# 8 MB loads with 64 KB runs and a written order on VectorE and GpSimd, in a decode attention kernel

## The chip, the cores and the metric

The kernel runs on one core of one Trainium2 chip. The metric is the device time of the program in microseconds (us); lower is better. Executions of the kernel before agree within 0.04%.

TensorE is called PE below, and its weight loads PEld; VectorE is DVE, ScalarE is ACT, GpSimd is POOL, and SyncE is SP. SP issues the loads. The 16 DMA engines of the core move the bytes. A run is a stretch of bytes in a row for one partition; the trace records it as one packet. Each load ends with 4-byte packets, the semaphore writes that signal its landing. A drain is a time in which fewer than 16 engines have a packet to move.

## The reference

One decode step of attention over a large cache, mixed with a small gated MLP. Cut to what matters:

```
B, H, Sk, Dh, D, F = 4, 32, 8192, 128, 1024, 3584
q = x @ wq                                     # (4, 1, 4096)
scores = einsum("bhqd,bhkd->bhqk", q, k_cache) * Dh**-0.5
p = softmax(scores)
o = einsum("bhqk,bhkd->bhqd", p, v_cache)
a = o.reshape(4, 1, 4096) @ wo
b = x + r * ((silu(x @ w_gate) * (x @ w_up)) @ w_down)
out = g * a + (1 - g) * b
```

The K and V caches are 268.4 MB each. All that is read comes to 575.68 MB, and every byte is used once, so the time is set by how fast bytes come in.

## The kernel before

K and V come in tiles of 4 MB: two heads, 128 partitions, 32 KB in a row for each partition. Five such tiles are in flight or in use, in a ring of five buffers. For K, VectorE transposes each tile in four chunks and PE multiplies each chunk with weights `Z` made from the query, eight matmuls a chunk, into `S_ps`. After eight tiles (16 heads) a softmax follows on VectorE, GpSimd and ScalarE. Its weights go to `PB`, and eight tiles later PE sums V with them, 32 matmuls a tile.

```
ring = ctx.enter_context(tc.tile_pool(name="ring", bufs=5))
ctx.enter_context(tc.manual_schedule(engines={mybir.EngineType.PE}))   # the others: the scheduler's order
...
def k_piece(u):
    ...
    kn = slot()                                          # 4 MB, the next of five
    nc.sync.dma_start(out=kn[:], in_=kv_view(A_k_cache, u))
    for c in range(JR // CJ):                            # 4 chunks
        T = ttp.tile([P, CJ, 2, 32, 2], BF, name="T", tag="T")      # two buffers
        nc.vector.transpose(out=T..., in_=kn[:, c * CJ * Dh:(c + 1) * CJ * Dh]...)
        for he in range(4):
            for z in range(2):
                nc.tensor.matmul(sps[:, z, :], lhsT=Z[:, he, s:s + P], rhs=T[...], ...)
        if c == 0:
            flush()                                      # finish an earlier group of heads
    if t == GT - 1:
        softmax(g)
...
def v_piece(u):
    ...
    cut = 4 if u == NT - 1 else 1                        # the last tile in four parts of 1 MB
    ...                                                  # 32 matmuls into o_ps
    nc.scalar.activation(out=o_sb[:], in_=o_ps[:, 0, :], func=ACT.Copy, scale=mE[:, 0:1])
    nc.vector.scalar_tensor_tensor(out=o_sb[:], in0=o_ps[:, 1, :], scalar=mE[:, 1:2], in1=o_sb[:], ...)
...
order: k0 ... k7, then k8 v0 k9 v1 ..., at the end v alone; 2 MB of wo before the last V tile, 6 MB after it
```

## Time and profile before

| | before |
|---|---|
| device time, median | 1349.33 us |
| span in the profile | 1347.8 us |
| PE busy / VectorE busy | 79% / 47% |
| DMA engines busy | 99.5% |

From the page of the kernel before: the span; busy us of each engine with its share of the span; busy tenths and GB/s of the DMA in 40 equal slices; packets, MB and engine share of the load queue; the chain of waits by engine.

```profile
span 1347.8 us, 8253 instructions
...
PE 1059.3 (79%) x4600; PEld 233.2 (17%) x2412; DVE 631.4 (47%) x375; ACT 41.5 (3%) x46; POOL 47.9 (4%) x115
...
DMA  9999999999999999999999999999999999999997
GB/s 403 433 433 422 433 430 430 432 433 430 430 433 430 430 431 434 429 431 432 433 428 432 433 430 430 433 431 429 432 434 429 428 433 434 429 428 434 432 423 323
...
q1 hardware_dynamic: 22104, 575.68, 99.5%
...
DMA 50%; PE 30%; DVE 11%; issue 6%; ACT 1%; POOL 1%; SPq 0%; DVEq 0%; ACTq 0%
```

DMA stands at 9 tenths or more in every slice but the last. Nothing else does. The queue is the bound, and the idle time of the other engines costs nothing as long as the queue has work.

The DMA issues of the same page: destination and source, number, KB each, and the median time from issue to landing.

```profile
piece<-in_A_k_cache_dram SPq DMA_DIRECT2D x64, 4096.0 KB, 39.4
piece<-in_A_v_cache_dram SPq DMA_DIRECT2D x63, 4096.0 KB, 39.1
```

A 4 MB load takes 9.8 us at this rate (4.19 MB / 428 GB/s), but 39 us pass from its issue to its landing. Four loads stand in the queue at any time. That depth is the margin which this kernel has against delays in the compute.

The timeline of VectorE at the end of one softmax group (start, duration, instruction; in brackets how long the engine had idled and for what):

```profile
780.80 0.24 DVE L355 SCALAR_TENSOR_TENSOR mex<-mask,m,pen 128x16 f32<-128x16 f32 x1
787.26 0.75 DVE L412 SCALAR_TENSOR_TENSOR OS<-o_ps,mE,OS 128x512 f32<-128x512 f32 x1 [6.23 <-ACT OS L411]
788.03 0.17 DVE L360 TENSOR_TENSOR gmm<-gmx,nmask 128x16 f32<-128x16 f32 x1
```

Between `mex` and `gmm`, both softmax steps, the scheduler has put the correction `OS` of a V sum, which waits for PE and ScalarE.

And the last work of PE in its timeline:

```profile
1342.57 1.02 PE L188 MATMUL acc<-piece,LT 128*4 128x512 bf16 x4 [0.17 <-DMA piece<-in_A_wo_dram]
...
1343.81 1.02 PE L188 MATMUL acc<-piece,LT 128*4 128x512 bf16 x4 [0.22 <-DMA piece<-in_A_wo_dram]
```

The last wo matmuls wait for their data: the load queue holds the end. The last packet lands at 1343.34 us, and PE is done 1.5 us after.

### The profile page before, as it was taken

The page shows a single profiled execution, that of the slowest core. Times are in us where ns is not written, and L with a number is a line of the kernel's source. Part 1 is how long each engine was busy: PE and PEld are TensorE (multiplying, and loading weights), DVE is VectorE, ACT ScalarE, POOL GpSimd, SP SyncE. Part 2 cuts the span into 40 slices and gives each one's busy share as a digit, 9 for nine tenths or more (in the row PEclk, how much of TensorE's full clock was granted, in tenths as well). Part 3 has the DMA queues.
Part 4 walks back from the last instruction along what each step waited for, and adds up shares of the span by engine and source line. Part 5 has one row for each costly group of instructions (what it writes and reads, how often), then busy time and mean ns, then how long its engine had stood idle before and what let it go on. Part 6 is the DMA issues. An engine that isn't in the chain of part 4 may idle for free.

```text
span 1347.8 us, 8253 instructions
## 1 busy us (share of the span) xinstructions
PE 1059.3 (79%) x4600; PEld 233.2 (17%) x2412; DVE 631.4 (47%) x375; ACT 41.5 (3%) x46; POOL 47.9 (4%) x115
## 2 busy tenths in 40 slices
PE   2667779876978868876998769888788859797878
PEld 0111111211111111111212111211112112121111
DVE  3555755535544554454545454444544456346000
ACT  0000010001000010001000010000000010000000
POOL 2000000000000000000000000000000000000000
PEclk8878989898989989989898879899888979999899
DMA  9999999999999999999999999999999999999997
GB/s 403 433 433 422 433 430 430 432 433 430 430 433 430 430 431 434 429 431 432 433 428 432 433 430 430 433 431 429 432 434 429 428 433 434 429 428 434 432 423 323
DMA packets 22162, 576.22 MB, mean 428 GB/s; under 512 B 2399, under 2 KB 2407, under 8 KB 2925
## 3 DMA queue, kind: packets, MB, share of 16 engines
q1 hardware_dynamic: 22104, 575.68, 99.5%
q8 instruction: 27, 0.44, 0.1%
q14 instruction: 11, 0.08, 0.0%
q10 hardware_dynamic: 20, 0.02, 0.0%
HBM read 575.68 MB, written 0.01 MB: 427 GB/s over the span
## 4 chain that ended last, share of the span: by engine, by line
DMA 50%; PE 30%; DVE 11%; issue 6%; ACT 1%; POOL 1%; SPq 0%; DVEq 0%; ACTq 0%
DMA piece<-in_A_k_cache_dram 40%; PE o_ps L401 16%; PE S_ps L342 13%; DVE T L336 10%; DMA piece<-in_A_v_cache_dram 9%; PE small L419 1%; DMA piece<-in_A_wo_dram 1%; POOL PB L373 1%; DVE PT L367 1%; ACT PTs L365 1%; ACT OS L411 1%; DVE OS L412 1%; POOL tot L377 0%; PE acc L188 0%; PE o_ps L225 0%
## 5 line engine op out<-in xcount | busy, mean ns | idle before, releaser
L336 DVE STREAM_TRANSPOSE T<-piece 128x2048 uint32<-128x2048 uint32 x256 | 576.1, 2288 | 437.0 <-DMA piece<-in_A_k_cache_dram 321.1
L342 PE MATMUL S_ps<-T,Z 128*128 128x512 bf16 x2048 | 544.6, 416 | 246.6 <-DVE T L336 235.3
L401 PE MATMUL o_ps<-piece,PB 128*16 128x512 bf16 x2048 | 457.6, 382 | 14.8 <-DMA piece<-in_A_v_cache_dram 14.8
L342 PEld LDWEIGHTS <-Z 128*128 128x128 bf16 x1024 | 108.0, 105 | 667.2 <-issue 664.3
L401 PEld LDWEIGHTS <-PB 128*16 128x16 bf16 x1024 | 91.9, 90 | 373.1 <-issue 361.3
L412 DVE SCALAR_TENSOR_TENSOR OS<-o_ps,mE,OS 128x512 f32<-128x512 f32 x16 | 12.0, 751 | 174.6 <-ACT OS L411 174.6
L326 POOL TENSOR_TENSOR Z<-qa,mq 128x16 bf16<-128x16 bf16 x64 | 16.7, 262 | 1072.3 <-PE S_ps L342 1054.3
L411 ACT ACTIVATE OS<-o_ps,mE 128x512 f32<-128x512 f32 x16 | 11.0, 687 | 1040.5 <-PE o_ps L401 1040.5
L419 PEld LDWEIGHTS small<-selg,OS 128*128 128x128 f32 x128 | 24.9, 273 | 12.2 <-issue 11.1
L419 PE MATMUL small<-selg,OS 128*128 128x8 f32 x128 | 22.3, 302 | 0.0
L353 DVE TENSOR_REDUCE m<-S_ps 128x1 f32<-128x1024 f32 x8 | 9.8, 1225 | 15.9 <-PE S_ps L342 15.9
L188 PE MATMUL acc<-piece,LT 128*4 128x512 bf16 x64 | 14.9, 378 | 1.7 <-DMA piece<-in_A_wo_dram 1.6
L373 POOL COPY PB<-PT 64x1024 bf16<-64x1024 bf16 x8 | 15.1, 1884 | 29.1 <-DVE rex L375 29.1
L372 ACT COPY PB<-PT 64x1024 bf16<-64x1024 bf16 x8 | 15.3, 1908 | 10.6 <-DVE PT L367 10.6
L367 DVE STREAM_TRANSPOSE PT<-PTs 128x1024 bf16<-128x1024 bf16 x8 | 10.0, 1245 | 11.9 <-ACT PTs L365 11.9
L188 PE MATMUL acc<-piece,hT 128*4 128x512 bf16 x56 | 12.4, 379 | 0.0
L131 PE MATMUL small<-identb,x 6*128 6x6 bf16 x8 | 0.6, 194 | 14.2 <-DVE identb L128 14.2
L379 DVE RECIPROCAL rinv<-tot 128x16 f32<-128x16 f32 x8 | 2.0, 253 | 19.9 <-POOL tot L377 19.9
L365 ACT ACTIVATE PTs<-S_ps,negm 128x1024 bf16<-128x1024 f32 x8 | 8.9, 1113 | 70.0 <-DVE negm L362 70.0
L225 PE MATMUL S_ps<-piece,xw 128*4 128x512 bf16 x64 | 6.6, 591 | 3.0 <-DMA piece<-in_A_wq_dram 3.0
L422 DVE SCALAR_TENSOR_TENSOR OT<-small,sgb,rinv 128x8 bf16<-128x8 f32 x16 | 3.2, 202 | 11.7 <-PE small L419 11.7
L358 POOL PARTITION_ALL_REDUCE gmx<-mex x8 | 3.1, 390 | 81.9 <-issue 50.3
(72 smaller groups left out, 74.6 us busy)
## 6 DMA issues: line engine op xcount, KB each, us to landing
piece<-in_A_k_cache_dram SPq DMA_DIRECT2D x64, 4096.0 KB, 39.4
piece<-in_A_v_cache_dram SPq DMA_DIRECT2D x63, 4096.0 KB, 39.1
piece<-in_A_wq_dram SPq DMA_DIRECT2D x2, 4096.0 KB, 22.1
piece<-in_B_w_gate_dram SPq DMA_DIRECT2D x2, 3584.0 KB, 40.1
piece<-in_B_w_up_dram SPq DMA_DIRECT2D x2, 3584.0 KB, 34.6
piece<-in_A_wo_dram SPq DMA_DIRECT2D x6, 1024.0 KB
piece<-in_B_w_down_dram SPq DMA_DIRECT2D x1, 4096.0 KB, 35.6
piece<-in_A_v_cache_dram SPq DMA_DIRECT2D x4, 1024.0 KB, 32.6
```

What stands on the lines that cost most here:

```text
L188: nc.tensor.matmul(out_ap, lhsT=lhsT, rhs=rhs, start=start, stop=True, skip_group_check=True)
L326: nc.gpsimd.tensor_tensor(out=Z[:, :, 31:31 + P].rearrange("p e (s d c) -> p e s d c", s=HT, d=QH)[:, :, :, :, 0], in0=qa[:, :, h0:h0 + HT ...
L336: nc.vector.transpose(out=T[:].rearrange("p j h i e -> p (j h i e)").bitcast(U32), in_=kn[:, c * CJ * Dh:(c + 1) * CJ * Dh].bitcast(U32))
L342: nc.tensor.matmul(sps[:, z, :], lhsT=Z[:, he, s:s + P], rhs=T[:, 16 * z:16 * z + 16, half, :, e], start=(t == 0 and c == 0 and he == 0), ...
L365: nc.scalar.activation(out=PTs[:], in_=sps[:].rearrange("p z n -> p (z n)"), func=ACT.Exp, bias=negm[:, 0:1], scale=scale, accum_out=rs[:, ...
L367: nc.vector.transpose(out=PT[:].rearrange("p j i -> p (j i)"), in_=PTs[:])
L372: nc.scalar.copy(out=Bv[0:W, :, :, 0, :], in_=Pv[0:W])
L373: nc.gpsimd.tensor_copy(out=Bv[W:P, :, :, 1, :], in_=Pv[W:P])
L401: nc.tensor.matmul(o_ps[row:row + NM, e, :], lhsT=B_[:, JT * t + c, z, w].rearrange("p e s j -> p (e s j)"), rhs=vn[:, j0 * Dh:(j0 + 4) * ...
L411: nc.scalar.activation(out=o_sb[:], in_=o_ps[:, 0, :], func=ACT.Copy, scale=mE[:, 0:1])
L412: nc.vector.scalar_tensor_tensor(out=o_sb[:], in0=o_ps[:, 1, :], scalar=mE[:, 1:2], in1=o_sb[:], op0=ALU.mult, op1=ALU.add)
L419: nc.tensor.matmul(oT[:, :], lhsT=o_sb[:, q * Dh:(q + 1) * Dh], rhs=selg[:, q].rearrange("p t s -> p (t s)"), start=(q == 0), stop=(q == 3))
```

## The change

The intent is longer runs. Two tiles become a pair of 8 MB, four heads with 64 KB in a row for each partition, loaded by one transfer. The ring stays at five slots of 4 MB, so one pair in five wraps round the end and comes as two 4 MB transfers with 32 KB runs. VectorE and GpSimd keep the written order, in which the softmax steps come before the V sum. The last V pairs come in halves, and w_down is laid out in longer runs.

```diff
-    ring = ctx.enter_context(tc.tile_pool(name="ring", bufs=5))
-    ctx.enter_context(tc.manual_schedule(engines={mybir.EngineType.PE}))
+    ctx.enter_context(tc.manual_schedule(engines={mybir.EngineType.PE, mybir.EngineType.DVE, mybir.EngineType.Pool}))
+    ring = const.tile([P, NS, RING], BF, name="ring")          # NS = 5
+    def load_pair(src, n, apart=False):
+        a = slots(2)
+        if a + 1 < NS and not apart:
+            lo = a * RING
+            nc.sync.dma_start(out=flat[:, lo:lo + 2 * n], in_=src)
+            return [flat[:, lo:lo + n], flat[:, lo + n:lo + 2 * n]]
+        halves = [ring[:, a], ring[:, (a + 1) % NS]]
+        for i, half in enumerate(halves):
+            nc.sync.dma_start(out=half[:, 0:n], in_=src[:, i * n:(i + 1) * n])
+        return halves
...
-    return cache[b, h0:h0 + HT].rearrange("h (r j) d -> (h r) (j d)", j=JR)
+    return cache[b, h0:h0 + NQ].rearrange("h (r j) d -> (h r) (j d)", j=2 * JR)
...                                                       # k_pair: 8 chunks
+            if n == 0:
+                flush()          # PE: 8 products that finish a group of heads
+            if n == 2:
+                flush_late()     # VectorE: their scaling
...                                                       # v_pair: 64 matmuls
+        if d < ND - 1:
+            vs = load_pair(vv, RING, apart=d >= ND - 3)
+        else:                                             # first half whole, second in four parts
+            vs = [ring[:, slots(1)] for _ in range(2)]
+            nc.sync.dma_start(out=vs[0], in_=vv[:, 0:RING])
+            for c in range(4):
+                lo, hi = c * RING // 4, (c + 1) * RING // 4
+                nc.sync.dma_start(out=vs[1][:, lo:hi], in_=vv[:, RING + lo:RING + hi])
```

Heads are now finished in groups of 16 instead of 8, so at the end four wo blocks instead of two need the last V sum.

## The prediction

> **What bounds the kernel now.** The load queue. The span is 1347.8 us; the table of DMA queues gives queue 1 575.68 MB and 99.5% of the 16 engines' span, and the 40-slice table shows DMA at 9 tenths or more in every slice but the last, mostly 428 to 434 GB/s. In the packet records all 16 engines are active together for 1272 us, and packet time per engine sums to 1341.7 us: hardly any transfer time is idle. PE is busy 79%, VectorE 47%. Issue to landing of a 4 MB K load is 39.4 us, against some 9.8 us of transfer (4.19 MB at 428 GB/s): four loads are queued, so compute has about three loads of margin. The waits of VectorE (321 us for K loads) and PE (235 us for VectorE) are slack.
>
> **What the change gives.** Bytes stay. Median packet times in the trace: 4 KB 160 ns, 8 KB 312 ns, 28 KB 1062 ns, 32 KB 1215 ns. The line through first and last has a slope of 27.2 B/ns per engine (435 GB/s for 16) and 9 to 10 ns per packet. The slope is the fabric ceiling that the Trainium skill gives (DMA: Bandwidth & Descriptors, "Where 436 GB/s comes from"). Longer runs can only remove the per-packet part. By the code, 52 of 68 pairs go as one 8 (or 7) MB transfer with runs of 64 or 56 KB; one pair in five wraps round the five-slot ring and keeps 32 KB, as do the last V pairs; w_down goes from 8 to 28 KB runs. About 7,300 of 22,100 packets vanish: 7,300 x 9.5 ns / 16 = 4.3 us, plus about 0.6 us for some 1,000 semaphore writes of 9 ns. All of it is critical, because the queue is. Gain about 4.9 us, 0.4%.
>
> **What it costs.** Buffering gets coarser. A pair takes about 19.6 us to load, and the next but one is issued only when the first half of the landed pair is read. K: four transposes at 2.29 us, 9 us, up to 12 where PE runs slow (8 score matmuls take 1.9 us, 3.4 at times). V: 7.0 us for 32 matmuls after what PE has left of K, some 8 to 14 us. So the margin falls from about 29 us to 5 to 10 us, but I expect no drain: PE needs about 17 + 14 us per K and V pair against 39.2 us of transfer. The softmax chain in written order (779.5 to 793.8 us in one group before, with a V correction in between) gets shorter, but lies in slack: worth about nothing. Start and tail stay: first loads at about 2.5 us, last landing to end 4 us.
>
> **Predicted: 1344.6 us**, range 1341 to 1350; faster by over 2% 0.01, within 2% 0.96, slower 0.03. Faster by 2% would need a rate over 435 GB/s.
>
> **Signs.** Right: queue 1 with about 14,800 packets, still over 99% of the span; 64 KB packets near 2420 ns; mean rate near 430 GB/s; issue to landing of 8 MB loads some 27 to 32 us; no slice of the middle below 9 tenths; PE and VectorE busy times unchanged. Wrong: slices below 425 GB/s, or VectorE and PE waiting for loads issued late, mean that the queue ran dry; 64 KB runs recorded as two packets of 1215 ns mean no gain.
>
> **What would upset it.** Drains in each softmax group from the thinner margin (3 us in each of 8 groups would cost 24 us, five times the gain), or slower reads with 64 KB between the partitions' runs.

## The result, and the profile after

| | before | after |
|---|---|---|
| device time, median (range) | 1349.33 us (1349.28 to 1349.45) | 1347.16 us (1346.62 to 1347.85) |
| ratio of the fast runs | | 0.9984 (95%: 0.9970 to 0.9998) |
| packets of the load queue | 22,104 | 13,976 |

A ratio is the mean time of one kernel's fast runs over that of the other's of the same rounds, so not quite the ratio of the medians. The verdict is "same" at 2%, as predicted, and the time lies inside the range. But the gain is 2.2 us, where 4.7 us were forecast. A second set of five runs (below) gave 1346.36 us, and the mean of all nine runs is 1346.9 us, so the gain is about 2.5 us: half of the forecast.

From the page of the changed kernel, the same lines as before:

```profile
span 1345.3 us, 7987 instructions
...
DMA  9999999999999999999999999999999999999997
GB/s 413 427 436 427 442 429 425 443 431 419 443 435 419 437 435 433 433 433 430 435 435 435 435 431 431 427 428 434 435 423 442 433 419 431 431 427 440 426 426 318
...
q1 hardware_dynamic: 13976, 575.68, 99.3%
...
DMA 58%; PE 23%; DVE 10%; issue 8%; ACT 0%; DVEq 0%; SPq 0%; POOL 0%
```

The queue is still full, and packets fell by 37%. The GB/s of a slice jump more than before, because a packet's bytes are counted in the slice in which it starts, and packets are now longer: a slice of 419 is no proof of an idle queue. The prediction had named slices under 425 as a sign of one, and that sign was badly chosen.

The DMA view of the changed kernel, its 8 MB K and V loads (no size is recorded for them; the last number is again the median from issue to landing):

```profile
ring<-in_A_k_cache_dram SPq DMA_DIRECT2D x25, 28.0
ring<-in_A_v_cache_dram SPq DMA_DIRECT2D x24, 29.3
```

An 8 MB load takes 19.4 us, so with 28 to 29 us from issue to landing only some 9 us of other work lie ahead of it in the queue. That is the coarser buffering that was predicted.

Where the gain is seen, and where it goes, is told by the packet records of the trace (one line for each packet: start, duration, size). This table is worked out from them. "Packet time" is the sum of all data packet durations of all queues, without the semaphore writes, divided by the 16 engines; "540 MB in" is when the load queue had brought that many bytes; "last landing" is the end of the last load.

```
kernel                 packet time   540 MB in   last landing   end of span   after the landing
before                    1341.7      1256.68      1343.34        1347.8           4.5
changed                   1337.5      1253.93      1340.68        1345.3           4.7
changed, again            1337.3      1253.54      1339.47        1344.1           4.6
```

Packet time fell by 4.2 us, nearly what was forecast. The stream gained 2.8 us by 540 MB and 2.7 us by the last landing, and 2.5 us reached the end. So the forecast lost its size between the packet durations and the clock.

Two lines of PE's timeline show that the end of the changed kernel has another owner:

```profile
1316.38 13.11 PE L429 MATMUL o_ps<-ring,PB 128*32 128x512 bf16 x60 [1.86 <-DMA ring<-in_A_v_cache_dram]
...
1335.32 7.07 PE L192 MATMUL acc<-ring,LT 128*4 128x512 bf16 x32 [0.36 <-DVE LT L291]
```

Sixty V matmuls of the last pair start at 1316.38 us, when a whole 4 MB half has landed. From there PE runs almost without a gap to the end of its 32 wo matmuls at 1342.4 us. Those no longer wait for their data. Load queue and PE now reach the end nearly together.

### The profile page after: what moved, and what is told of

It reads as the page before. It is cut to its first block, busy times and chain, and to the rows that moved or that the text cites. A ratio compares the mean times of both kernels' runs of the same rounds, so it can differ in the third digit from the quotient of the medians.

```text
span 1345.3 us, 7987 instructions
## 1 busy us (share of the span) xinstructions
PE 1050.1 (78%) x4536; PEld 229.2 (17%) x2348; DVE 623.1 (46%) x358; ACT 51.4 (4%) x46; POOL 59.0 (4%) x91
## 3 DMA queue, kind: packets, MB, share of 16 engines
q1 hardware_dynamic: 13976, 575.68, 99.3%
## 4 chain that ended last, share of the span: by engine, by line
DMA 58%; PE 23%; DVE 10%; issue 8%; ACT 0%; DVEq 0%; SPq 0%; POOL 0%
DMA ring<-in_A_k_cache_dram 50%; PE S_ps L358 11%; PE o_ps L429 11%; DVE T L352 10%; DMA ring<-in_A_v_cache_dram 5%; DMA ring<-in_B_w_gate_dram 3%; PE small L448 1%; PE acc L192 1%; PE o_ps L226 0%; ACT OS L441 0%; DVEq L352 0%; DVE OS L442 0%; ACT res L495 0%; SPq L109 0%; POOL Z L335 0%
## 5 line engine op out<-in xcount | busy, mean ns | idle before, releaser
L352 DVE STREAM_TRANSPOSE T<-ring 128x2048 uint32<-128x2048 uint32 x256 | 570.6, 2282 | 501.4 <-DMA ring<-in_A_k_cache_dram 425.9
L429 PE MATMUL o_ps<-ring,PB 128*32 128x512 bf16 x2048 | 460.5, 387 | 37.6 <-DMA ring<-in_A_v_cache_dram 37.6
L429 PEld LDWEIGHTS <-PB 128*32 128x32 bf16 x1024 | 100.7, 99 | 395.2 <-issue 373.1
L335 POOL TENSOR_TENSOR Z<-qa,mq 128x16 bf16<-128x16 bf16 x32 | 8.3, 262 | 808.4 <-PE S_ps L358 737.3
L394 POOL COPY PB<-PT 32x1024 bf16<-32x1024 bf16 x16 | 30.4, 1897 | 26.8 <-DVE rex L396 26.5
L392 ACT COPY PB<-PT 32x1024 bf16<-32x1024 bf16 x16 | 30.6, 1914 | 10.7 <-DVE PT L385 10.6
L192 PE MATMUL acc<-ring,LT 128*4 128x512 bf16 x64 | 14.5, 379 | 0.7 <-DVE LT L291 0.7
L448 PEld LDWEIGHTS small<-selg,OS 128*128 128x128 f32 x64 | 11.8, 260 | 7.0 <-issue 4.9
L192 PE MATMUL acc<-ring,hT 128*4 128x512 bf16 x56 | 12.2, 379 | 0.0
L448 PE MATMUL small<-selg,OS 128*128 128x16 f32 x64 | 10.6, 302 | 0.9 <-DVE OS L442 0.9
```

The costliest lines, as they stand in the source:

```text
L192: nc.tensor.matmul(out_ap, lhsT=lhsT, rhs=rhs, start=start, stop=True, skip_group_check=True)
L335: nc.gpsimd.tensor_tensor(out=Z[:, :, QP - 1:QP - 1 + P].rearrange("p e (q c) -> p e q c", c=QP)[:, :, :, 0], in0=qa[:, :, h0:h0 + NQ, b], ...
L352: nc.vector.transpose(out=T[:].rearrange("p j h i e -> p (j h i e)").bitcast(U32), in_=kn[:, c * CJ * Dh:(c + 1) * CJ * Dh].bitcast(U32))
L392: nc.scalar.copy(out=Bv[at, :, :, q, :], in_=Pv[at])
L394: nc.gpsimd.tensor_copy(out=Bv[at, :, :, q, :], in_=Pv[at])
L429: nc.tensor.matmul(o_ps[row:row + NM, e, :], lhsT=B_[:, RD * t + c, z, w].rearrange("p e s j -> p (e s j)"), rhs=vn[:, j0 * Dh:(j0 + 4) * ...
```

## The experiments

Twelve runs were made, all correct, one of them of the changed kernel again. They came in three calls, each on another chip; in each call the kernel before ran on the same chip, and its medians (1349.42, 1349.45 and 1349.42 us) differ by 0.03 us, so runs of different calls are compared below. The theories:

- **A**: the packets do save some 4.5 us, and about half is lost to lag of one DMA engine at the end and to short drains of the queue.
- **B**: a packet simply costs half of what was thought.
- **C**: not the runs but the written order gives the gain.
- **D**: in the changed kernel PE holds the end.
- **E**: work placed early in a K pair delays the next load and drains the queue.

### The changed kernel again

No edit.

> The changed kernel once more, for a second trace. Theory A (64 KB runs save about 11 ns for each pair of 32 KB packets, some 4.5 us in all, and about half of that is lost to what one DMA engine has fallen behind the others at the end, plus short drains): 1346.6 to 1348.0 us, packet time per engine near 1337.5 us, and the time from the median engine's last landing to the last engine's between 1 and 3 us, differing from the first trace's 2.6 us. Theory B (the forecast was simply too high: a packet costs half of what was thought): same time, but the packet times would have to differ between traces.

Measured: 1346.36 us median (1345.83 to 1347.91), packet time 1337.3 us. In the profiled run the last DMA engine finished 2.0 us after the median of the 16; in the first trace it was 2.9 us (2.6 us as the expectation counted it), and in the kernel before 1.8 us. Packet times of the two traces repeat to 0.2 us while the last landing differs by 1.2 us, of which 0.4 us is there when 540 MB are in. Between these two traces the variation comes from the end and from drains, not from the packets. The sign that was named for theory B, packet times that differ between traces, did not appear.

### 32 KB runs in 8 MB transfers

```diff
-    ring = const.tile([P, NS, RING], BF, name="ring")
+    ring = const.tile([P, NS, RING + 32], BF, name="ring")   # 64 B between slots: no run passes a slot
```

> 8 MB transfers kept, but every slot padded by 64 B so that each run is 32 KB again. Theory A: packet time per engine back to about 1342 us, total 1350.5 to 1352.5 us, slower than the kernel before, because the coarser loads and the late engine stay. Theory B (run length is worth only 2 us): 1349.0 to 1349.8 us. Theory C (the written order of VectorE and GpSimd gave the gain): stays at 1347.

Measured: 1348.34 us median, but from 1347.72 to 1351.61. The packet time is 1340.6 us. This misses A, which wanted 1350.5 or more, and B by a little, and it rules out C in its simple form, since the time did not stay at 1347. The spread was the new fact. The profiled run was the slowest one, and its trace shows where its time went. PE timeline of that run, the same two places as above:

```profile
1317.92 16.04 PE L451 MATMUL o_ps<-ring,PB 128*32 128x512 bf16 x60 [3.53 <-DMA ring<-in_A_v_cache_dram]
...
1339.79 7.07 PE L213 MATMUL acc<-ring,LT 128*4 128x512 bf16 x32 [0.36 <-DVE LT L312]
```

The sixty V matmuls took 16.04 us here against 13.11 us before them in the changed kernel. The windows view gives the granted clock for the stretch from 1316 to 1332 us; after the busy times of PE, PEld, DVE, ACT and POOL come PEclk, DMA share and GB/s. First this run, then the changed kernel:

```profile
1316.00:1332.00 16.00, 14.08 (x52) 2.87 (x26) 0.00 (x0) 0.00 (x0) 0.00 (x0) 0.79 1.01 421
```

```profile
1316.00:1332.00 16.00, 14.71 (x73) 3.35 (x36) 0.75 (x1) 0.69 (x1) 0.00 (x0) 1.00 1.01 421
```

The clock was 0.79 here and 1.00 there, and the difference that the traces show ahead of it is the idle time of PE: 3.53 us here, 1.86 us there. The same holds in all profiles with this form of end:

```
kernel (this end)         idle before the last V pair   granted clock 1316-1332   from last landing to end
changed                         1.86 us                        1.00                     4.7 us
changed, again                  1.86                           1.00                     4.6
finishing products later        1.88                           1.00                     4.6
halves                          3.56                           0.89                     6.2
halves, scheduler's order       3.61                           0.79                     7.4
8 MB loads, 32 KB runs          3.53                           0.79                     7.6
pairs, scheduler's order        3.54                           0.79                     7.3
```

The Trainium skill describes this: in "TensorE: Matmul & The Clock Gate", section "What's actually happening", the array falls back to half clock after an idle window of about 3.4 us and needs about as long to recover. The traces agree with the half clock and with its length: the clock records show 0.5 for 3.41 us in "halves" and for 6.83 us in the three kernels with 0.79. They do not agree that a gap must be that long. An earlier V pair of the changed kernel:

```profile
1301.69 7.89 PE L429 MATMUL o_ps<-ring,PB 128*32 128x512 bf16 x28 [2.69 <-DMA ring<-in_A_v_cache_dram]
```

After this gap of 2.69 us the clock was 0.5 from 1302.25 to 1305.66 us, while in the kernel before a gap of 2.65 us, which ended at 1294.5 us, kept the full clock. So at this place 1.9 us of idle did no harm, 3.5 us lost the clock, and gaps between them did either. 3.41 us at half clock cost 1.7 us of work and 6.83 us cost 3.4 us (estimates from these records), and the ends are 1.5 to 3 us longer than in the kernels with the full clock. No run here changed the length of that gap alone.

### All pairs in halves

```diff
-        if a + 1 < NS and not apart:
+        if False:
```

> All pairs loaded as two 4 MB transfers with 32 KB runs, order of the engines kept. Theory A: packets back, margin of the queue partly back: 1349.3 to 1351.5 us. Theory B: 1349.0 to 1349.8 us. Theory C: stays at 1347.

Measured: 1350.82 us (1350.56 to 1351.81), 1.4 us slower than the kernel before. Its stream is no slower (540 MB in at 1256.20 us against 1256.68). Its end is: 6.2 us from the last landing to the end against 4.5, with the clock at 0.89. The number fell in A's interval, but for D's reason: pairs in halves are slower than the kernel before because of the end, not because of the margin.

### Only PE in written order

```diff
-    ctx.enter_context(tc.manual_schedule(engines={mybir.EngineType.PE, mybir.EngineType.DVE, mybir.EngineType.Pool}))
+    ctx.enter_context(tc.manual_schedule(engines={mybir.EngineType.PE}))
```

> Only PE in written order, VectorE and GpSimd left to the scheduler as before. Theories A and B: no change beyond 0.7 us, 1346.5 to 1348 us, since the softmax chain lies in slack. Theory C: 1349 us or more.

Measured: 1356.16 us (1354.68 to 1357.79), 9 us slower than the changed kernel (means 1356.0 and 1346.9). A and B are plainly wrong here, and C is right that the order matters, though not as where the gain comes from. (VectorE and GpSimd were given back to the scheduler together; the run does not part them.) Timeline of this run at the end of a softmax group, DVE lines and the issue of the next load by SP:

```profile
311.23 0.23 DVE L373 SCALAR_TENSOR_TENSOR mex<-mask,m,pen 128x16 f32<-128x16 f32 x1
...
324.60 0.75 DVE L442 SCALAR_TENSOR_TENSOR OS<-o_ps,mE,OS 128x512 f32<-128x512 f32 x1 [13.14 <-ACT OS L441]
325.27 0.17 DVE L378 TENSOR_TENSOR gmm<-gmx,nmask 128x16 f32<-128x16 f32 x1
...
332.93 4.44 DVE L352 STREAM_TRANSPOSE T<-ring 128x2048 uint32<-128x2048 uint32 x2
...
346.05 0.33 SPq L109 DMA_DIRECT2D ring<-in_A_k_cache_dram  x1
```

And the same place in the changed kernel:

```profile
311.53 0.23 DVE L373 SCALAR_TENSOR_TENSOR mex<-mask,m,pen 128x16 f32<-128x16 f32 x1
...
312.33 0.17 DVE L378 TENSOR_TENSOR gmm<-gmx,nmask 128x16 f32<-128x16 f32 x1 [0.57 <-POOL gmx L376]
...
324.91 0.75 DVE L442 SCALAR_TENSOR_TENSOR OS<-o_ps,mE,OS 128x512 f32<-128x512 f32 x1 [4.79 <-ACT OS L441]
328.06 4.51 DVE L352 STREAM_TRANSPOSE T<-ring 128x2048 uint32<-128x2048 uint32 x2 [2.40 <-DMA ring<-in_A_k_cache_dram]
...
341.40 0.33 SPq L109 DMA_DIRECT2D ring<-in_A_k_cache_dram  x1
```

In the scheduler's order the correction `OS`, which waits 13 us for a V sum, stands ahead of the softmax step `gmm`. The rest of the softmax comes after it. VectorE is free only at 332.93 us for a K pair that had landed some 6 us before, and the next load is issued at 346.05 us instead of 341.40. The packet records show fewer than 16 engines at work from 343.9 to 347.4 us: 2.0 us of the whole queue. There are four such drains, at 344, 657, 972 and 1129 us, of 1.1 to 2.3 us each, 7.4 us in all. The kernel before had the same order (`OS` between `mex` and `gmm` in its lines above) and paid nothing, as it had four loads in the queue.

### The end rearranged

Theory D: let PE start on the last V pair earlier.

```diff
-        if (kind, d) == ("v", ND - 1):
-            for g in range(2):
-                wo_block(g)()                        # 2 MB of wo ahead of the last V pair
...
-            nc.sync.dma_start(out=vs[0], in_=vv[:, 0:RING])
+            for c in range(2):                       # its first half in two parts
+                lo, hi = c * RING // 2, (c + 1) * RING // 2
+                nc.sync.dma_start(out=vs[0][:, lo:hi], in_=vv[:, lo:hi])
...
-    last = [wo_block(g) for g in range(2, NWB - 2)]
+    last = [wo_block(g) for g in range(NWB - 2)]
```

> The changed kernel with its end rearranged: the first half of the last V pair comes in two pieces and before the first two blocks of wo, so that PE can start on it about 5 us earlier. Theory D (in the changed kernel the end is held by PE, not by the load queue: 64 V matmuls can start only when a whole 4 MB half has landed, and where the granted clock is low there the end slips by up to 3 us): the last wo matmul again ends about 1.5 us after the last landing, as in the kernel before; 1345.2 to 1346.8 us, with less spread between runs. Rival (the queue alone holds the end): no change, 1346.4 to 1347.4 us.

Measured: 1347.06 us, from 1345.59 to 1348.93. The first half of D holds: from last landing to end it is 4.4 us with the clock at 1.00. The second half fails: neither median nor spread improved. The median lies where the rival theory, that the queue alone holds the end, had it. The profiled run was again the slowest; its last engine finished 4.6 us after the median one and 3.0 us after the fifteenth, and there were short drains at 499 and 927 us.

### The same, with the finishing products later

Theory E. In the changed kernel, this is a K pair that starts a new group (timeline, all engines but PEld):

```profile
1106.94 4.51 DVE L352 STREAM_TRANSPOSE T<-ring 128x2048 uint32<-128x2048 uint32 x2 [3.13 <-DMA ring<-in_A_k_cache_dram]
...
1109.40 3.57 PE L358 MATMUL S_ps<-T,Z 128*128 128x512 bf16 x8 [7.10 <-DVE T L352]
...
1112.77 1.72 PE L448 MATMUL small<-selg,OS 128*128 128x16 f32 x8
...
1117.94 6.70 DVE L352 STREAM_TRANSPOSE T<-ring 128x2048 uint32<-128x2048 uint32 x3 [2.48 <-PE S_ps L358]
...
1120.28 0.33 SPq L109 DMA_DIRECT2D ring<-in_A_k_cache_dram  x1
```

The pair has landed at 1106.5 us. PE had idled 7.1 us and the granted clock is 0.50 now, so its first chunk takes 3.57 us in place of 1.89. Then come the eight products (`small`) that finish the heads of an earlier group, 1.72 us, and the transposes wait, since they have two buffers. Only after the fourth transpose, at 1120.28 us, is the next load issued. The load in progress lands at 1125.9 us, which looks like 5 us of margin. But the 16 engines are not level: the first of them had done its part of that load 6.0 us before the last. So the first engines ran dry from 1119.8 to 1121.5 us; the missing packets come to 0.34 us of the whole queue. With a packet's bytes spread over its duration, the rate between 1100 and 1150 us was 423.4 GB/s against about 432 in its neighbours, 1 us lost. But only some 0.7 us of this lies at the drain (403.6 GB/s from 1120 to 1130 us); the rest lies at 1100 to 1110 us, before the late load.

```diff
-            if n == 0:
+            if n == 4:
                 flush()
-            if n == 2:
+            if n == 6:
                 flush_late()
```

> The same, and the four 8-matmul products that finish a group of heads put after the fifth chunk of a K pair instead of after the first. Theory E (the short drain near 1120 us comes from this work delaying the first half of a K pair): no drain over 0.1 us of engine mean after 5 us, and 0.3 to 1.2 us faster than the run with the tail alone. Rival (drains do not matter, fast DMA engines only wait for the slow one): no difference, within 0.3 us.

Measured, with both edits: 1345.88 us (1345.70 to 1346.09), ratio to before 0.9973 (0.9959 to 0.9987). It is the fastest kernel here and as steady as the kernel before. Its load is issued 10.6 us after VectorE starts on the pair in place of 13.3 us, and drains shrink to under 0.1 us, except those of the very end. Its end is again held by the load queue:

```profile
1320.58 1.89 PE L431 MATMUL o_ps<-ring,PB 128*32 128x512 bf16 x8 [0.41 <-DMA ring<-in_A_v_cache_dram]
...
1340.44 1.02 PE L192 MATMUL acc<-ring,LT 128*4 128x512 bf16 x4 [0.22 <-DMA ring<-in_A_wo_dram]
```

The last V matmuls start at 1320.6 us, not in one block from 1316 on, and the last wo matmuls wait for their data as in the kernel before.

### The finishing products later, alone

> The changed kernel with only the finishing products of a head group moved from after the first to after the fifth chunk of a K pair; its end as it was. Theory E (these products hold the first half of a K pair, and with it the next load): most of the gain of the run with both edits, 1345.7 to 1346.6 us, and little spread. Theory D (the end held by PE matters too): up to 1 us slower than both edits together, with some runs near 1348 us. If neither: 1346.8 us as the changed kernel.

Measured: 1347.99 us median, from 1345.93 to 1349.39. So neither edit alone helps, and both together give 1 us and a narrow spread. The profiled run (1346.87 us) still had a drain of 0.2 us at 1120 us though its load was issued 2.5 us earlier, because the first DMA engine was 6.2 us ahead of the last. Theory E is therefore not proved by itself. Steady and unsteady kernels ran side by side on two of the chips, so the chip is not the reason. The slow runs of the two single edits were mostly not profiled, and which of drain, engine lag and clock made each of them slow stays open.

### Run length alone: 32 and 16 KB with the rearranged kernel

The slots were padded by 64 B after each 32 KB, or after each 16 KB, of K and V, as in the 32 KB experiment above.

> The rearranged end with 32 KB runs again (8 MB transfers, slots padded by 64 B). With the end no longer held by PE, the difference to the run with 64 KB runs is that of the run length alone. If packet durations add up as the forecast took them: 4.2 us slower than it. If, as the rates inside the traces show (431.0 against 432.5 GB/s with a drain of about 1 us), less is real: 2 to 3.3 us slower.

> The same with 16 KB runs of K and V. A cost of 9 to 10 ns for each packet, added up, makes it 9 to 10 us slower than the 32 KB one, packet time per engine about 1350 us. If only 60 per cent of that is real, as for the step from 64 to 32 KB: 5 to 6.5 us slower.

> Both edits with 32 KB runs, 8 MB transfers kept. Without drains or a late end the difference to the same kernel with 64 KB runs (1345.9 us) is that of some 6,700 packets. At 6 ns each, as the times at which 540 MB had landed give it: 2.3 to 2.9 us slower, 1348.2 to 1348.8 us. At the 9.5 to 11 ns of the packet durations: 4 to 4.6 us slower, 1349.9 us or more.

Measured: 1347.88 us (rearranged end, 32 KB), 1354.75 us (rearranged end, 16 KB) and 1347.89 us (both edits, 32 KB). The clean pair is both edits with 64 KB and with 32 KB, since both are steady:

```
runs            packets   packet time   540 MB in   last landing   mean of 5 runs
64 KB (4 of 5)   14,120      1337.1       1253.24      1339.96        1345.87 us
32 KB            20,776      1340.4       1255.41      1341.71        1347.86
16 KB            36,904      1350.9       1261.84      1348.91        1354.80   (without the second edit)
```

From 32 to 64 KB, 6,656 packets less save 1.99 us, or 4.8 ns each (1.99 us x 16 / 6,656). This is under both expectations, and half of the 9 to 10 ns of the forecast. From 16 to 32 KB it is 6.94 us for 16,128 packets, 6.9 ns each; against the 32 KB kernel with the same end (1348.10 us in the mean) it is 6.70 us, 6.6 ns each. So the 16 KB step came out near the smaller expectation (5 to 6.5 us), and the rearranged end at 32 KB was 1.1 us slower than its unsteady 64 KB partner, less than either expectation. The packet durations say more (3.3 and 10.5 us) than the clock. The 16 KB run shows why they cannot be added: 1348.7 us of packet time per engine on the load queue fit into the 1346.7 us between the first packet and the last. The records of neighbouring packets on one engine overlap.

How much they overlap can be read from the packet records. More than 16 records are open at once for 37 us with 64 KB runs, 57 us with 32 KB and 117 us with 16 KB. If each packet is matched with the one whose end lies nearest to its start (the records do not name the engine), the next record starts about 3.5 ns before the last one ends. From start to start it is 2423.8 ns in the mean for 64 KB, 1214.2 for 32 KB and 610.5 for 16 KB. Two short packets less one long one give 4.6 and 6.8 ns, which is what the clock gave.

The Trainium skill leads to a lower figure than the forecast's. "DMA: Bandwidth & Descriptors", section "Why small descriptors are slow (HBM only)", gives a fixed overhead of about 3 cycles a packet and 32 B of descriptor data. If a recorded packet is one such packet, and the cycles are those of the 850 MHz fabric of the same page, that is an estimate of 3.5 + 1.2 = 4.7 ns (at the 27.2 B/ns of the traces). The runs give 4.8 ns at the step to 64 KB, but 6.6 to 6.9 ns at the step from 16 to 32 KB, so the close match at the first step may be luck.

### Halves with the scheduler's order

The two edits "all pairs in halves" and "only PE in written order" together, the fourth corner.

> All pairs in two 4 MB halves and VectorE and GpSimd left to the scheduler: the fourth corner beside the changed kernel (1346.8), the same with the scheduler (1356.2) and halves in written order (1350.8). Theory: the written order is needed only because an 8 MB pair leaves little margin; halves free and ask for slots one by one, so the scheduler's order costs at most 3 us here, 1350 to 1354 us. Rival (the scheduler's order costs its 9 us anywhere in this kernel): 1359 us or more.

Measured: 1351.72 us (1351.09 to 1352.21).

| | written order | scheduler's order |
|---|---|---|
| 8 MB pairs | 1346.9 | 1356.0 |
| 4 MB halves | 1351.0 | 1351.6 |

(means of all runs). With halves the order is worth 0.6 us, and the traces show no drain in the middle of either; with 8 MB pairs it is worth 9.1 us. So the written order is what makes the coarser loads affordable. By itself it is nearly worthless.

### Four slots instead of five

```diff
-    NS = 5
+    NS = 4
```

> A ring of four slots instead of five: no pair wraps, all runs 64 KB, but a pair can be asked for only when both halves of the one before the last are read. Theory (margin): K needs about 18 us of the 19.6 us until the next pair has landed, more where PE is slow, so the queue drains at most K pairs; 1355 to 1420 us. If only packets counted: 1346 us or a little less.

Measured: 1446.29 us (1442.53 to 1450.42), beyond what was expected. Page, and SP's timeline in the middle:

```profile
DMA  9999998999899899999998988989999999999998
GB/s 410 432 378 425 389 405 379 407 407 426 358 393 390 380 403 426 391 387 398 407 405 379 434 379 378 405 380 407 405 408 407 403 381 407 383 401 434 389 427 349
...
q1 hardware_dynamic: 12104, 575.68, 93.8%
```

```profile
1004.25 0.33 SPq L109 DMA_DIRECT2D ring<-in_A_k_cache_dram  x1
1020.12 0.33 SPq L109 DMA_DIRECT2D ring<-in_A_v_cache_dram  x1
1045.89 0.33 SPq L109 DMA_DIRECT2D ring<-in_A_k_cache_dram  x1
```

It has the fewest packets of all and is 7% slower. The time from one K load's issue to the next is 41.6 us, where 16.8 MB (a K and a V pair) need 38.8 us at full rate. The queue drains once in each K and V period, about 80 us over the run. Packets count for a few us, margin for a hundred.

## Why the prediction was right or wrong

**The bound: right.** DMA was busy 99.5% before and 99.3% after, and every experiment that idled the queue cost time. The range and the packet count (13,976 against "about 14,800", which had left the semaphore writes in) held, and 64 KB packets do take 2419 ns.

**The size of the gain: wrong by a factor of two. The step that failed is "About 7,300 of 22,100 packets vanish: 7,300 x 9.5 ns / 16 = 4.3 us".** The packets vanished and their recorded time fell by 4.2 us. But the clock gave 4.8 ns for a vanished packet: an estimate of 7,300 x 4.8 / 16 = 2.2 us. The intercept of a line through packet durations is not the cost of a packet to the stream, since the records of neighbouring packets overlap by about 3.5 ns; from start to start the traces give 4.6 ns. Theory B was right about most of the gap, though not about its sign; theory A was right about the rest.

**"But I expect no drain": wrong in small.** The margin of 5 to 10 us was right for the median engine. But the 16 engines were 5 to 6 us apart by 1100 us (5.0 us in the kernel before, too), and a drain starts with the first of them. One such place cost some 0.7 us in the first profile.

**"Start and tail stay": right in time, wrong in cause.** 4.7 us from last landing to end looks like the 4.5 us before. But PE holds the end now, with 60 V and 32 wo matmuls nearly in line, and the kernels with 1.7 us more of PE idle time ahead of them lost the clock and ended up to 3 us later.

**"Worth about nothing" for the softmax order: wrong.** It is worth 9.1 us with 8 MB pairs, because without it the queue drains. It was judged in the kernel before, where the margin hides it, and not in the kernel that was predicted. In the 4 MB form it is worth 0.6 us, so there the sentence would have stood.

**What adds up.** With the drains and the end mended, the kernel is 3.6 us faster than before (1349.45 to 1345.88). Of this, 2.0 us is shown to be run length. The 32 KB version of the mended kernel is still 1.5 us faster than the kernel before: it has 1,328 fewer packets and semaphore writes, which at the packet times is an estimate of under 1 us; what the rest is was not taken apart.

**What stays open.** Which of drain, engine lag and clock makes the slow runs of the changed kernel slow, run by run, and why only both edits together remove the spread.

## What to carry to other kernels

When a stream already runs at the limit of the DMA engines, longer runs are worth a few ns per packet: measure it by swapping the run length alone, not by adding up packet durations. Larger loads spend queue depth, so count the margin from the first DMA engine that finishes, and check that nothing with a long wait stands ahead of work which frees a buffer; the same order can be free with four loads queued and cost 9 us with two. And look at who owns the end: a PE gap of 3.5 us just before the last burst of matmuls went with an end up to 3 us longer here, as much as the whole change gained.

## What the Trainium skill lacked or had wrong

- "DMA: Bandwidth & Descriptors", "Rules for kernel authors", asks for 128 partitions and at least 1 MiB per DMA, and gives no figure for the run length of transfers above that. Here, with 8 MB transfers kept, going from 16 to 32 KB runs gave 6.7 to 6.9 us and from 32 to 64 KB 2.0 us of 1350.
- The same page, "Why small descriptors are slow (HBM only)", leads to an estimate of 4.7 ns a packet, if its cycles are taken at 850 MHz: near the 4.8 ns at 32 to 64 KB, too low at 16 to 32 KB (6.6 to 6.9 ns). No page says that recorded packet durations overlap (by about 3.5 ns a packet; 1348.7 us of packet time in a stretch of 1346.7 us).
- The same page says that the engines of one DMA finish independently, but not how far they drift in a long stream: 5 to 6 us between the first and the last engine by 1100 us here, about a third of an 8 MB load.
- "Runtime: NRT & Kernel Launch", "Instruction fetch mechanics", has instructions fetched in blocks of 16 KiB, but not what that takes from a full load queue. In every trace 27 packets of 16 KB are on a queue marked "instruction", of about 1.07 us each in the kernel before and the changed one, and during almost every one of them 15 instead of 16 packets of the load queue were under way. By these figures that is an estimate of 1.8 us of the whole queue.
- "DMA: Bandwidth & Descriptors", "Measured (HBM→SBUF, 128 partitions, SWDGE, issued from GpSimd)", tops out at 425 GB/s for a 16 MB transfer. The streams here, issued from SP, held 430 to 431 GB/s in the kernel before (32 KB runs) and up to 433 in the changed one (mostly 64 KB), over 50 us stretches from 900 to 1300 us.
- "TensorE: Matmul & The Clock Gate", "What's actually happening", names an idle window of about 3.4 us. Less was enough here: half the clock was lost after a gap of 2.69 us (in the 3.41 us before 1302.25 us of the changed kernel PE was busy for 0.72 us), and after 3.5 us; it was kept after 1.9 us.
